# New order lists and buffer places for a fused attention and gated feed-forward kernel on one core

## The chip, the cores and the metric

The kernel runs on one core of a Trainium2 chip. A core has five engines, each with its own instruction queue that runs in order: TensorE (matrix products), VectorE, ScalarE, GpSimd (called POOL in the profile) and SyncE (SP). They wait for each other through semaphores. Transfers between HBM and the on-chip memory SBUF run on 16 DMA engines that all queues share; here POOL and SP issue nearly all of them. Products are written to PSUM, a small memory of 8 banks per partition. The metric is the device time of one execution in microseconds (us); the figure compared is the median over runs.

## The reference

The first half is causal attention, the second a gated feed-forward layer on its result. Cut to what matters:

```python
# q, k, v: [4 batches, 8 heads, 768 tokens, 64]
scores = np.matmul(q, k.transpose(0, 1, 3, 2)) / 8
# heads 0, 2, 6 see all earlier keys; the other five see the
# first 4 keys ("sinks") and the last 64
scores = np.where(mask, scores, -1e9)
a = softmax(scores)
x = np.matmul(a, v)          # as [3072 tokens, 512 features]

g, val = x @ w_gate, x @ w_val            # 512 -> 1536
ffn = (gelu(g) * val) @ w_out             # 1536 -> 512
out = x + sigmoid(x @ w_res) * ffn        # float32 [3072, 512]
```

Inputs are float32; the kernel works in float16 with float32 sums in PSUM.

## The kernel before

**Chunks.** The 3072 tokens are six chunks of 512 (`CHUNKS`); chunks 1 and 4 take the end of one batch and the start of the next. Each chunk goes through loads of q, k and v, a transpose of q and k to put features on partitions, attention scores, exponentials and masks, the weighted sum of v, a transpose of the result, the gate and value products for 12 blocks of 128 hidden features, and output products. The kernel has no loop at run time: every instruction of every chunk is written out, and chunks overlap, so that the attention of one chunk runs between the output products of the one before.

**Transfers.** POOL issues the loads of q, k, v and the weights, which convert to float16 on the way, and for chunks 1 to 4 the stores that add the feed-forward result to `out` (L1523). In the first stages (`loads_rows`) q and k are transposed by TensorE with the identity matrix `ident` (L825). From chunk 2 on (and for four tiles of batch 1) `loads_natural` brings 128 tokens of q or k into a staging buffer `qks` and SP issues a DMA transpose of it (task `dT`, L869), and two copies `q6` (L880) put one head pair on other partitions. For the windowed heads the values are needed a second time, shifted by 64 tokens: that copy `vs` is issued by SP (L774) once the value tiles `va` have landed. From chunk 3 on, half of the attention result is transposed by an SP transpose too (task `xD`, L1217, into `xT`); TensorE transposes the other half (L1226). The attention result itself is stored by SP in one transfer of 1 MB per chunk (`xst`, L1444), before POOL adds to it. The loads of the first chunk come in halves of 256 tokens: of the first half, heads 0 to 3 and 4 to 7 of k and q are four transfers, of the second half k and q are one each.

**Products.** Gate, value and output products use a scheme with seven sub-products in place of eight; their partial sums are added on VectorE (`merge`, `plus`, `s1` to `s4`) and copied by VectorE or ScalarE (`keep`, `seed`, `hold`). A gate or value product of 512 tokens and 512 features is split at its half (`g0`, `v0` and so on, two 512-wide matmuls each): the first half needs the part of `xT` that TensorE transposed, the second half the part that `xD` brings. From the second half of the program on, many products stand as two half-wide matmuls of 64 columns (line L617, the other form is L616). Score tasks (L1013, L1104) and the windowed products (L1137) are blocks of up to 16 small matmuls on parts of the array, and the weighted sums of v (65 columns wide) are small as well.

**The order.** Each piece of work is a task with an engine, a duration in a simple table, dependencies and buffers. A planner (`Graph.schedule`) could place tasks by priority, but here it follows the string `PLAN`. It holds, separated by "/", five lists of task numbers, one for each engine in the order TensorE, ScalarE, VectorE, POOL, SP, and a sixth list that fixes for every buffer which slot (or PSUM bank) it takes, -1 for free choice:

```python
queue = {e: [self.tasks[x] for x in xs] for e, xs in zip(ENGS, lists)}
...
for b, x in zip(bufs, lists[5]):
    b.fixed = x if x >= 0 else None
```

Some tasks may run on more than one engine; the list in which their number stands decides. The planner still walks through modelled time. For a DMA it takes the end as

```python
t.end = dma_free[here] + 1.6 + t.late
```

where `late` is an allowance set where the task is made. In the modelled times where TensorE has nothing to do before the first gate product `g0`, the planner inserts matmuls of a blank tile (task `warm`, L1579 of the profile); they compute nothing that is used. `assign_waits` then gives each task the semaphore waits that its dependencies and the earlier users of its buffers need, and `emit` writes the instructions in the planned order.

Of the kernel before, what the change touches and what calls it, by code (L numbers as in the profile page):

```python
# [54 lines left out]
    "230 242 228 234 408 411 238 232 236 422 240 459 425 414 426 462 427 464 428 432 419 476 467 433 434 442 443 444 445 "  # L55
    "449 451 450 473 440 471 438 457 479 480 481 455 252 482 486 487 488 496 497 498 499 530 522 514 492 503 505 504 494 "
    "538 515 523 509 531 511 546 539 548 558 552 519 534 560 554 518 559 561 553 555 547 570 527 549 526 572 576 542 543 "
    "266 264 250 535 564 566 565 578 567 588 589 582 584 583 590 585 591 676 621 577 579 610 571 573 690 612 613 679 667 "
    "670 614 623 615 616 624 617 672 674 687 625 626 636 696 627 697 692 698 693 699 694 695 628 640 641 683 685 703 704 "
    "705 638 646 714 647 715 713 718 716 717 711 722 709 642 643 724 723 652 653 649 650 730 734 728 655 658 656 741 659 "  # L60
    "740 736 735 742 743 746 737 748 747 749 753 774 785 752 777 754 755 796 788 779 780 799 790 791 782 758 793 801 760 "
    "759 807 802 804 761 818 810 764 829 812 821 766 832 765 823 815 834 813 826 767 824 837 848 835 931 850 852 922 924 "
    "853 854 855 858 859 906 910 861 864 862 865 926 928 867 868 870 871 912 914 881 882 877 934 935 936 937 917 920 933 "
    "938 887 888 879 942 944 943 956 952 953 883 957 958 884 959 954 955 950 948 963 965 964 893 890 894 891 969 971 899 "
    "900 896 897 987 981 975 977 976 978 988 983 982 984 989 1015 990 993 995 999 1018 1026 1037 1020 1001 1029 994 1040 "
    "1021 1023 1032 1031 1042 996 1043 1034 1045 1048 1000 1002 1006 1070 1059 1051 1008 1073 1062 1005 1053 1007 1064 1075 "
    "1056 1065 1067 1054 1078 1089 1166 1076 1091 1163 1093 1094 1153 1156 1095 1099 1100 1096 1105 1106 1102 1103 1147 "
    "1151 1111 1112 1108 1109 1159 1161 1118 1168 1169 1170 1122 1173 1171 1172 1177 1123 1179 1178 1120 1184 1185 1186 "
    "1128 1187 1188 1189 1129 1124 1190 1191 1125 1195 1197 1196 1134 1135 1131 1132 1201 1203 1140 1137 1141 1138 1207 "
    "1208 1210 1209 1213 1219 1221 1220 1222 1247 1215 1214 1216 1250 1226 1269 1258 1252 1253 1225 1261 1255 1272 1227 "  # L70
    "1263 1264 1274 1280 1266 1237 1277 1275 1283 1228 1291 1239 1302 1294 1285 1231 1305 1296 1286 1288 1297 1299 1307 "
    "1233 1308 1310 1321 1402 1232 1234 1238 1240 1385 1323 1325 1326 1379 1383 1327 1331 1332 1328 1399 1387 1337 1338 "
    "1334 1335 1343 1390 1393 1344 1405 1406 1407 1340 1354 1355 1408 1404 1409 1341 1395 1397 1360 1361 1413 1415 1414 "
    "1356 1424 1357 1425 1420 1421 1426 1422 1427 1423 1366 1367 1363 1364 1431 1432 1433 1372 1369 1370 1373 1439 1437 "
    "1350 1449 1450 1443 1444 1445 1446 1456 1451 1452 1461 1483 1455 1463 1486 1494 1457 1488 1458 1497 1462 1464 1505 "
    "1489 1499 1491 1500 1508 1467 1502 1469 1516 1510 1511 1468 1519 1527 1513 1521 1470 1522 1524 1530 1538 1473 1475 "
    "1541 1474 1532 1476 1533 1535 1543 1352 1640 1544 1546 1557 1559 1631 1633 1561 1562 1563 1564 1567 1568 1570 1621 "
    "1623 1571 1573 1574 1635 1637 1576 1577 1579 1580 1615 1619 1590 1591 1586 1626 1629 1643 1644 1596 1597 1645 1646 "
    "1642 1647 1651 1652 1653 1588 1658 1659 1660 1662 1663 1664 1665 1661 1592 1593 1669 1671 1670 1602 1603 1599 1600 "
    "1677 1675 1608 1609 1605 1680 1704 1686 1606 1681 1688 1682 1692 1683 1705 1687 1693 1689 1694 1720 1695 1731 1706 "  # L80
    "1723 1707 1742 1734 1699 1725 1745 1736 1726 1728 1737 1701 1698 1739 1700 1747 1753 1748 1750 1710 1756 1764 1712 "
    "1775 1767 1758 1759 1778 1769 1711 1761 1780 1781 1713 1770 1772 1783 1825 1827 1829 1798 1830 1799 1831 1800 1801 "
    "1832 1835 1836 1804 1805 1838 1839 1807 1841 1808 1842 1844 1845 1813 1814 1847 1848 1794 1810 1811 1796 1816 1817 / "
    "198 229 409 412 237 423 424 460 415 416 465 463 420 477 478 468 226 441 472 474 227 439 513 524 516 532 495 253 512 "
    "540 562 556 520 550 536 528 574 544 267 251 568 580 586 592 258 677 622 611 691 260 680 668 671 261 675 673 688 637 "
    "702 644 684 686 648 639 712 710 645 721 731 729 738 744 750 775 786 756 787 797 798 783 784 762 808 805 806 819 820 "
    "830 1442 831 768 733 828 827 849 932 851 923 925 860 907 911 927 929 913 915 878 918 921 880 941 889 886 949 962 951 "
    "970 972 313 979 985 991 311 1016 997 1027 1038 1028 1025 1024 1003 1047 1046 1049 1071 1072 1061 1009 1069 1068 1090 "
    "1167 1092 1097 1154 1101 1098 1157 1164 1148 1152 1160 1119 1162 1126 1176 1121 1130 1127 1194 1202 1206 365 1211 1223 "
    "1248 1217 1249 1259 1257 1256 1229 1281 1282 1278 1279 1292 1293 1303 1304 1241 1301 1300 1235 1322 362 1403 1386 1324 "  # L90
    "1329 1380 1384 1330 1388 1400 1391 1394 1358 1396 1398 1362 1412 1359 1430 1679 1440 1351 1447 1453 1485 1465 1495 "
    "1459 1496 1506 1493 1492 1471 1517 1518 1515 1514 1529 1539 1540 1477 1536 1537 1353 1641 1558 1560 1632 1566 1634 "
    "1622 1624 1638 1636 1616 1620 1627 1587 1630 1650 1589 1598 1595 1668 1676 1684 1690 1696 1721 1732 1708 1733 1743 "
    "1730 1729 1702 1754 1752 1751 1765 1776 1777 1714 1773 1774 1828 1826 974 1833 1802 1834 1837 1803 1806 1795 1853 1797 "
    "/ 0 15 16 14 17 1 231 243 235 233 239 410 241 224 225 11 413 461 429 13 430 417 418 431 466 421 435 436 446 452 447 "
    "453 437 470 469 448 458 456 454 475 483 489 484 490 485 500 501 506 493 507 502 491 525 12 510 594 517 533 541 595 508 "
    "563 557 521 596 551 545 265 529 598 599 569 537 600 593 587 259 602 601 603 678 575 581 605 632 633 669 606 618 604 "
    "635 681 609 682 689 700 701 629 634 706 607 707 708 719 608 630 720 725 726 654 651 619 727 663 657 664 770 597 660 "
    "771 739 745 772 751 665 776 778 773 789 781 792 800 757 794 803 795 809 763 811 661 814 822 833 825 836 816 769 817 "
    "840 839 838 841 844 842 856 845 857 843 846 847 863 909 866 874 869 875 908 872 885 930 916 939 940 919 945 946 947 "  # L100
    "960 961 966 967 895 892 968 898 1013 1011 1012 901 903 980 986 1014 904 1017 992 1019 312 310 1022 1030 1039 1041 1033 "
    "1044 998 1035 1036 1004 1050 1060 1052 1074 1063 1055 1066 1077 1010 1057 1058 1081 1080 1079 1085 1082 1086 1084 1088 "
    "1083 1087 1107 1155 1104 1115 1116 1149 1150 1110 1113 1158 1174 1175 1180 1181 1165 1182 1192 1193 1198 1199 1136 "
    "1133 1204 1144 1145 1200 1139 1243 1244 1212 1246 1142 364 1245 1224 1218 1251 1270 1271 1254 1260 1262 1273 1265 1276 "
    "1267 1268 1230 1284 1295 1287 1306 1298 1290 1309 1289 1312 1311 1317 363 1236 1318 1242 1313 1314 1316 1320 1333 1315 "
    "1319 1339 1382 1336 1389 1348 1381 1347 1392 1410 1411 1342 1401 1416 1417 1428 1429 1368 1365 1434 1435 1371 1438 "
    "1436 1418 1479 1481 1374 1480 1448 1454 1484 1345 1487 1482 1490 1460 1498 1466 1501 1507 1509 1503 1504 1512 1520 "
    "1528 1523 1472 1526 1525 1531 1542 1534 1478 1549 1545 1550 1377 1376 1548 1551 1547 1553 1565 1554 1552 1555 1569 "
    "1556 1572 1575 1583 1578 1581 1584 1639 1618 1594 1617 1625 1628 1648 1649 1654 1655 1656 1666 1667 1672 1673 1604 "
# [460 lines left out]
def build_kernel(nc, q, k, v, w_gate, w_val, w_out, w_res, out):  # L570
# [153 lines left out]
    def values(b, a, z, base, each, on_engines=False):  # L724

        BB = batch(b)
# [23 lines left out]
        if on_engines:  # L750
            ts = []
# [18 lines left out]
        for lo in cuts:  # L770
            hi = lo + 1 if each else z
            ts = []
            for dst, src, off in ((0, 64, 1), (64, 0, 0)):
# [5 lines left out]
                if on_engines:  # L779
                    ts[-1].late = 1.5  # L780
# [3 lines left out]
    def loads_rows(c, si, b, a, z):  # L784

        BB = batch(b)
# [58 lines left out]
    def loads_natural(c, si, b, a, z):  # L845
# [8 lines left out]
        for i in range(a, z):  # L854
            for j, src in ((1, k), (0, q)):
# [9 lines left out]
                for d in ds:  # L865
                    d.late = 3.5
# [814 lines left out]
```

## Time and profile before

| what | value |
|---|---|
| median of 3 runs | 267.65 us (265.87 to 273.2) |
| the profiled execution | 270.48 us, of it 268.7 us span |
| TensorE busy | 255.6 us, 3434 matmuls |
| VectorE busy | 206.6 us |
| ScalarE busy | 165.6 us |
| POOL busy | 106.6 us, DMA issues included |
| HBM | 29.36 MB read, 10.49 MB written |
| granted TensorE clock, mean | 0.991 |

The span runs from the first to the last instruction; the device time of the same execution is 1.8 us longer. The profile lists groups of instructions by line and tile, the waits of each engine with what ended them, a chain of work that ended last, a timeline, and windows with the busy time of each engine. Lines such as L1217 are those of the kernel before. "PEclk" is the granted clock, 1.00 being full. The queue q0 holds what POOL issued, q1 what SP issued, and q8 the fetches of instructions. "issue" in a wait is time in which an engine waited for no semaphore.

### The profile page before, as it was taken

To read this page: it belongs to the slowest core of one execution; us is meant where nothing else is said; L and a number is where in the kernel's file an instruction comes from. 1 tells how busy PE (TensorE), PEld (TensorE's weight loads), DVE (VectorE), ACT (ScalarE), POOL (GpSimd) and SP (SyncE) were. 2 spreads that over 40 slices of the span, in tenths; PEclk is the share of its full clock that TensorE was granted. 3 is DMA by queue.
4 is the path that set the end of the run, shared out by engine and by line. 5 is a ranking of instruction groups with operands and counts; after the bars stand their busy time and mean duration, and the time that the engine had idled before them with its cause. 6 is when DMAs were issued, how large, how long until landed. Compare 5 with 4: busy or idle time off the path is not lost.

```text
span 268.7 us, 8098 instructions
## 1 busy us (share of the span) xinstructions
PE 255.6 (95%) x3434; PEld 180.5 (67%) x3434; DVE 206.6 (77%) x454; ACT 165.6 (62%) x293; POOL 106.6 (40%) x145
## 2 busy tenths in 40 slices
PE   7899999989999999999999699999999997999992
PEld 5568564458577578577678267589587676778891
DVE  2696566887888978778988567988788985768985
ACT  2588456874655986655886246897365996346421
POOL 8999729803130992769229510001030030110022
PEclk9999999999999999999999799999999999999999
DMA  7999999998989999999909999347473019340004
GB/s 70 171 188 207 181 205 203 157 164 91 166 211 124 165 135 153 115 174 254 168 11 132 169 217 150 72 55 83 165 90 82 2 16 127 46 56 2 2 2 156
DMA packets 102067, 33.17 MB, mean 123 GB/s; under 512 B 88720, under 2 KB 97168, under 8 KB 102032
## 3 DMA queue, kind: packets, MB, share of 16 engines
q0 software_dynamic: 74704, 18.88, 77.2%
q1 hardware_dynamic: 27184, 13.65, 28.6%
q8 instruction: 27, 0.44, 0.7%
q10 hardware_dynamic: 144, 0.13, 0.1%
q14 instruction: 8, 0.07, 0.1%
HBM read 29.36 MB, written 10.49 MB: 148 GB/s over the span
## 4 chain that ended last, share of the span: by engine, by line
PE 70%; DMA 14%; POOL 11%; ACT 2%; issue 2%; DVE 1%; POOLq 0%; DVEq 0%
PE ps L617 32%; PE ps L616 31%; DMA va<-in_v_dram 8%; POOL qks L678 4%; PE ps L1013 3%; DMA xT<-x 3%; DMA vs<-va 3%; POOL va L678 2%; PE ps L1137 1%; POOL wo L678 1%; PE ps L1226 1%; POOL wg L678 1%; POOL wv L678 1%; POOL m_win L636 0%; ACT L1111 0%
## 5 line engine op out<-in xcount | busy, mean ns | idle before, releaser
L1523 POOL DMA_DIRECT2D out_dram<-otile x16 | 14.9, 1014 | 87.8 <-DVE otile L1519 77.6
L616 PE MATMUL ps<-xT,wg 128*128 128x512 f16 (+1 forms) x172 | 40.1, 344 | 0.0
L616 PE MATMUL ps<-xT,wv 128*128 128x512 f16 (+1 forms) x162 | 37.2, 341 | 2.2 <-DMA xT<-x 2.2
L1292 ACT ACTIVATE gact<-ps 128x512 f16<-128x512 f32 x38 | 22.5, 597 | 25.7 <-PE ps L616 17.7
L1294 DVE SCALAR_TENSOR_TENSOR hT<-gact,ps 128x512 f16<-128x512 f16 x38 | 25.8, 685 | 15.0 <-PE ps L616 9.8
L678 POOL DMA_DIRECT2D qks<-in_q_dram x37 | 30.4, 855 | 16.4 <-DMA qT<-qks 8.9
L678 POOL DMA_DIRECT2D qks<-in_k_dram x37 | 31.4, 873 | 10.4 <-DMA kT<-qks 10.4
L678 POOL DMA_DIRECT2D va<-in_v_dram x24 | 23.8, 1014 | 17.0 <-PE ps L1226 11.9
L1366 DVE TENSOR_TENSOR ps<-ps,otile 128x256 f32<-128x256 f32 x60 | 24.7, 429 | 7.2 <-PE ps L616 3.4
L1384 ACT ACTIVATE gact<-ps 128x512 f16<-128x512 f32 x30 | 16.4, 595 | 15.8 <-PE ps L616 8.6
L616 PEld LDWEIGHTS ps<-xT,wv 128*128 128x128 f16 x162 | 15.8, 99 | 14.4 <-DMA xT<-x 2.7
L616 PEld LDWEIGHTS ps<-xT,wg 128*128 128x128 f16 x172 | 16.8, 99 | 10.8 <-issue 1.1
L1029 ACT ACTIVATE ea<-ps 128x1024 f16<-128x1024 f32 (+2 forms) x24 | 21.4, 920 | 3.2 <-PE ps L1013 3.2
L1391 DVE SCALAR_TENSOR_TENSOR hT<-gact,ps 128x512 f16<-128x512 f16 x30 | 19.7, 683 | 1.8 <-PE ps L617 0.7
L617 PE MATMUL ps<-xT,wv 128*64 128x512 f16 (+1 forms) x164 | 20.1, 346 | 0.0
L616 PE MATMUL ps<-wo,hT 128*128 128x256 f16 (+1 forms) x114 | 19.2, 296 | 0.2 <-ACT otile L1490 0.2
L1463 ACT ACTIVATE srs<-ps 128x512 f32<-128x512 f32 x22 | 12.9, 596 | 8.3 <-PE ps L617 7.0
L617 PE MATMUL ps<-xT,wg 128*64 128x512 f16 (+1 forms) x144 | 17.7, 344 | 0.0
L1204 DVE TENSOR_TENSOR xtok<-ps,rcp 128x512 f32<-128x512 f32 (+1 forms) x28 | 16.9, 610 | 0.7
L1495 DVE TENSOR_TENSOR otile<-otile,ps 128x256 f32<-128x256 f32 x33 | 13.6, 417 | 4.6 <-PE ps L617 2.4
L1013 PE MATMUL ps<-qT,kT 64*128 64x64 f16 (+4 forms) x391 | 16.6, 213 | 0.0
L1362 ACT ACTIVATE ps<-ps 128x256 f32<-128x256 f32 x26 | 9.6, 370 | 9.5 <-PE ps L616 6.3
(174 smaller groups left out, 593.5 us busy)
## 6 DMA issues: line engine op xcount, KB each, us to landing
out_dram<-xtok SPq DMA_DIRECT2D x4, 1024.0 KB, 6.3
out_dram<-otile POOLq DMA_DIRECT2D x16, 256.0 KB, 6.0
va<-in_v_dram POOLq DMA_DIRECT2D x24, 128.0 KB, 7.6
qks<-in_k_dram POOLq DMA_DIRECT2D x32, 64.0 KB, 7.6
qks<-in_q_dram POOLq DMA_DIRECT2D x32, 64.0 KB, 7.1
wv<-in_moe_w_val_dram POOLq DMA_DIRECT2D x3, 512.0 KB, 11.3
wg<-in_moe_w_gate_dram POOLq DMA_DIRECT2D x3, 512.0 KB, 7.7
wo<-in_moe_w_out_dram POOLq DMA_DIRECT2D x4, 384.0 KB, 19.7
```

The source lines that it names most:

```text
L616: return e.matmul(o, lhsT=lhsT, rhs=rhs, **k)
L617: return [e.matmul(o[h:h + 64], lhsT=lhsT[:, h:h + 64], rhs=rhs, **k) for h in (0, 64)][-1]
L678: return G.add(eng, issue, lambda e: e.dma_start(out_ap(), in_ap), deps, prio, bufs=bufs, dma=cost, name=name, grp=grp)
L1013: return [e.matmul(at(scr)[:, oo:oo + w], lhsT=side(BB, qb, low, 1)[half, k0:k0 + 128], rhs=side(BB, qb, low, 0)[half, qq:qq + w], start=T ...
L1029: return e.activation(out=o, in_=i_, func=AF.Exp, scale=SM_SCALE)
L1204: t2 = G.add("dve", c_dve(2 * n * 64), lambda e: e.tensor_tensor(out=xview(), in0=avv(0, DHEAD), in1=scale(), op=ALU.mult), [t1] + xdeps, ...
L1292: ta = G.add("act", c_act(512), (lambda gb=gb, ga=ga, gw=gw: lambda e: e.activation(out=at(ga)[:, :], in_=at(gb)[:, gw], func=AF.Gelu))(), ...
L1294: th = G.add("dve", c_dve(512), (lambda vb=vb, ga=ga, f=f, vw=vw: lambda e: e.scalar_tensor_tensor(out=hv(f), in0=at(ga)[:, :], scalar=0.5 ...
L1366: return G.add("dve", c_dve(256), lambda e: e.tensor_tensor(out=at(ps)[:, o], in0=at(ps)[:, BL], in1=at(es)[:, 0:256], op=ALU.add), deps, ...
L1384: ta = G.add("act", c_act(512), (lambda x=x, ga=ga, both=both: lambda e: e.activation(out=two(at(ga)[:, :]), in_=both(x), func=AF.Gelu))() ...
L1391: th = G.add("dve", c_dve(512), (lambda x=x, f=f, ga=ga, both=both: lambda e: e.scalar_tensor_tensor(out=two(hv(f)), in0=two(at(ga)[:, :]) ...
L1523: t = G.add("pool", 1.0, (lambda ot=ot, r0=r0: lambda e: e.dma_start(out[r0:r0 + 128, :], at(ot)[:, :], accum_op=ALU.add))(), ends + [stor ...
```

## The change

The string `PLAN` is replaced, all five lists and the places. Nine values of `late` are raised or set:

```diff
 PLAN = (
-    "230 242 228 234 408 411 238 232 236 422 240 459 425 414 426 462 427 464 428 432 419 476 467 433 434 442 443 444 445 "
...
 )
...
-            BB.vtok[i].late = (0.3 if base < -40 else 1.2) if base < 50 else 4.0
+            BB.vtok[i].late = (1.2 if base < -40 else 1.6) if base < 50 else 4.5
...
-                if on_engines:
-                    ts[-1].late = 1.5
+                ts[-1].late = 2.5
...
-                    t.late = 1.0 if c else 0.0
+                    t.late = 1.0 if c else 0.7
...
-                    d.late = 3.5
+                    d.late = 4.5
...
-                t.late = 1.0
+                t.late = 2.5
...
-            t.late = 1.0
+            t.late = 2.0
...
-        t.late = 2.5 if c == 2 else 1.0
+        t.late = 3.0 if c in (2, 3) else 1.5
...
-        stored[c].late = 1.0
+        stored[c].late = 2.5
...
-                t.late = 2.0 if c < 4 else 1.5
+                t.late = 3.5 if c < 4 else 2.5
```

From the top these belong to the value loads, the shifted copies `vs`, the first loads of q and k, the later loads of q and k, the transposes `dT`, the copies `q6`, the transposes `xD`, the stores `xst` and the accumulating stores. The code of the first loads, with its halves of 256 tokens, is the same in both versions; their order is not. Before, the first six were q of the second half, then q and k of the first half's heads 0 to 3, q and k of its heads 4 to 7, and k of the second half. After, k of the second half comes first, then k, q, k, q of the first half and q of the second. In the new lists 11 more tasks stand on ScalarE and 11 fewer on VectorE, one add of the last chunk stands on POOL, and the program has 68 blank matmuls instead of 70. All lines of the kernel after `PLAN` have numbers lower by one.

## The prediction

> **What bounds the kernel now.** I read the page first, then TensorE's waits, the chain of waits, and around each place that these name the timelines, the windows and the DMA queues. The page's first table and TensorE's own waits:
>
> ```profile
> PE 255.6 (95%) x3434; PEld 180.5 (67%) x3434; DVE 206.6 (77%) x454; ACT 165.6 (62%) x293; POOL 106.6 (40%) x145
> ```
> ```profile
> PE ps L616 <- DMA xT<-x: 2.2, 1, 2.2
> PE ps L1137 <- issue: 2.0, 1, 2.0
> PE ps L1137 <- DMA vs<-va: 1.3, 1, 1.3
> ```
>
> TensorE is the bound: 255.6 of 268.7 us. Three waits make 5.5 us of its idle time; the rest lies before the first load has landed and after the last product. An order of work cannot shorten the products, only these waits. The chain of waits says where they stand (start, us, what):
>
> ```profile
> 31.15 21.46 DMA va<-in_v_dram
> 52.62 7.84 DMA vs<-va
> ...
> 141.83 8.45 DMA xT<-x
> 150.32 9.89 PE ps L616 x50
> ...
> 226.09 1.96 issue
> ```
>
> Wait A, at 59.2: the last value load issued at 31.15 lands at 52.6, its shifted copy takes 7.84, and the windowed product starts at 60.5. Wait B, at 148.1: the DMA transpose xD, issued at 141.83, lands after 8.45 us; TensorE had come to its reader 2.2 us earlier. Wait C, at 225.9: TensorE waits for nothing that has a semaphore. TensorE's timeline there, and the DMA queues from 225.5 to 229:
>
> ```profile
> 225.89 0.19 PE L1137 MATMUL ps<-vs,es 128*64 128x65 f16 x1
> 228.04 0.19 PE L1137 MATMUL ps<-va,es 128*64 128x65 f16 x1 [1.96 <-issue]
> ```
> ```profile
> q8 instruction: 1, 0.02, 1.6%
> ```
>
> A block of sixteen small products stops in its middle while one instruction block is fetched. The windows show what came before it (us, PE busy (x matmuls), clock), beside another dense stretch that ran without a stop:
>
> ```profile
> 181.00:184.62 3.62, 3.62 (x137) 1.00 0.54 55
> 222.66:225.90 3.24, 3.24 (x141) 1.00 1.06 160
> ```
>
> Wait B has a second price. The window after it (PEclk stands behind the POOL pair):
>
> ```profile
> 151.40:154.90 3.50, 3.50 (x10) 1.29 (x9) 2.24 (x5) 1.19 (x2) 0.95 (x2) 0.51 1.72 231
> ```
>
> The clock is at half. In the timeline five groups of two 512-wide products take 3.84 us there (151.20 to 155.04) and 0.435 each elsewhere: 3.84 - 5 x 0.435 = 1.7 us lost. So B costs 2.2 + 1.7 = 3.9.
>
> **What the change does to the program.** I read the orders of both built programs. The planner's lists decide everything: with the new lists and the old values of `late` the emitted program is the new one but for the blank matmuls (70 instead of 68). The nine edits of `late` have therefore no effect at run time of their own. TensorE has the same 732 real tasks; six change between whole and column-halved form. Giving every task its time from this trace (without its waits) the real and blank work adds to 251.6 us before and 251.4 after, 0.2 for two blank matmuls of 0.11. Eleven more tasks stand on ScalarE and eleven fewer on VectorE (293 and 443, from 282 and 454); at 62% and 77% busy both have room. The chains product - ScalarE or VectorE - product are equally tight: in 41 places before and 45 after, less than 0.2 us of other work covers them. I charge 0.5 for these.
>
> *Wait A.* On POOL's queue the four value loads of this stage stand 34th, 37th, 40th and 41st after, and 31st, 43rd, 44th and 46th before. Loads land one behind the other here (the queue carries 189 GB/s from 31 to 53). Two `wo` loads, which landed 1.9 us apart, and two of q and k at 0.3 to 0.5 go behind them: adding the gaps in the new order, the last lands near 47.6, five earlier. With the same 7.84 for the copy that is 55.5, against a need at 59 to 60. Gain 1.3. What is late next are those two `wo` loads: the same sum puts them at 49.4 and 51.4; their readers, at 51.8 and 52.2 before, stand 0.9 us of work later, so nothing waits. If POOL were 4 us later, A would be back.
>
> *Wait B.* From xD's last producer to its first reader TensorE had 7.6 us of work and now has 10.2, because seven first halves of gate and value products go ahead of it instead of two. TensorE asked 6.3 us after xD's issue; now 8.9, against a landing of 8.45: 0.45 to spare. Beside xD, POOL issued eleven loads and four accumulating stores between 139.6 and 155.6; the new list leaves eight loads and four stores there, the other loads going ahead into an idle stretch of POOL (10.1 us before 139.6). So the landing should be shorter. I take the whole 3.9; if it lands 2.6 us later than now, 0.
>
> Here the skill has a rule. "TensorE: Matmul & The Clock Gate", section on HAM oscillation: the clock is halved after idle gaps longer than about 3.4 us. The row shows half clock after 2.2 us of idling. By the rule B is worth 2.2, and any new wait under 3.4 us costs its length alone; by the row B is worth 3.9 and a new wait of 2 us costs up to 3.7. I go by the row, in both directions.
>
> *Wait C.* The densest 128 products in a row take 2.77 us of work before (ending in the stop) and 3.43 after. The second densest stretch before, inside the window 181.00:184.62, also has 3.43, and it did not stop. By these rows C is gone: 2.0. The skill's rule speaks against this part: "Runtime: NRT & Kernel Launch", section on instruction fetch mechanics, says that a block's fetch runs ahead of execution and is mostly hidden; then spreading small products gains nothing. By the rule 0, by the row 2.0. I take 1.6, since 3.43 passed once, on another alignment to the blocks.
>
> *Start.* The first six loads change order (k before q), each with the same 0.73 to 0.95 us issue on POOL; one large load still goes first, and the first transpose still waits for `ident`, written at 6.73. VectorE's ones for the value tiles are done by 2.7, so the value loads' new wait for them costs nothing. Gain 0.2, the two blank matmuls; bounds -1.3 (three gate tasks of 0.43, now ahead of the second half's weighted values, entering idle time) and +1 (a late small load).
>
> *New: the transposes behind xD.* Before, one transpose of the next chunk (of q or k, L869) was ahead of xD on SP's queue and seven behind it until its last reader. Now all eight, and two of the chunk after, stand behind. SP's timeline in this stage:
>
> ```profile
> 143.12 1.87 SPq L869 DMA_TRANSPOSE kT<-qks  x1
> 148.04 0.39 SPq L1444 DMA_DIRECT2D out_dram<-xtok  x1
> 148.48 2.16 SPq L869 DMA_TRANSPOSE qT<-qks  x1
> 150.68 4.04 SPq L869 DMA_TRANSPOSE kT<-qks  x1
> ```
>
> The seven took 2.0 us each on average there (1.2 to 4.05) and landed 4.9 to 11.7 after issue. With A gone xD is issued at 140.5; ten transposes end at 140.5 + 1.25 + 20.2 = 161.9, so the last is issued at 159.9 and, at the seven's mean of 9.1, lands at 169.0. Its reader, a score task, stands 29.9 us of TensorE work behind xD's issue: 170.4. Spare 1.4. For relief, the 1 MB store xst (L1444), between them before, moves behind all of these. Every later product queues behind that score task. Charge 0.5; bounds 0 and, at 2.5 us each (4.8 later, 3.4 of wait, 1.7 of clock), 5.
>
> *End.* One add moves to POOL (0.7) and an output issue stands on ScalarE ahead of a tanh; the add it waits for ends about 0.5 us before that tanh's products do. The last two products and the adds behind them are the same. 0, bounds 0 to +0.5.
>
> **Sum.** The profiled execution took 270.48 (span 268.7 and 1.8 around it): 270.5 - 1.3 - 3.9 - 1.6 - 0.2 + 0.5 + 0.5 = 264.5. Some 0.5 for landings that no row shows gives 265.0. That execution is 2.8 above the median of 267.65 and 4.6 above the fastest, so other runs lack some of A, B and C; the program without them is the same one, and I leave 265.0.
>
> **Rivals.** *The waits are that execution's own.* The fastest run, 265.87, has at most 3 us of the 7.2. Where the median lacks B's 3.9, the change brings 267.65 - 1.3 - 1.6 + 1.5 = 266. For it: the spread of 7.3 us between three runs. With a wait of 2 us and its half clock in the new order it ends at 266 + 3.7 = 269.7. Chance 0.25. *All clean.* Every gain and neither charge, with the start's 1.3: 270.5 - 7.2 - 1.3 = 262.0. Chance 0.12. *Slower.* SP's row of ten transposes: if each takes 3.2 us instead of 2.0, the last comes 12 us later, the score task waits 10.6 us and pays 1.7 of clock: 264 + 12.3 = 276. It decides from 2.9 us each (a wait of 7.3, 273). For it: one took 4.05 in this stage; against it: two took 1.2, and the big store that stood among them is gone. Chance 0.13. The likeliest, near 265: 0.50.
>
> **The numbers.** A measurement of this kernel tells 2% (5.4 us) from no change: 262.3 and 273.0. Faster by more comes from the clean case alone, 0.12; slower 0.13; between 0.75. The range reaches from the clean case, 262.0, over the new wait of the first rival to 271: below it some 0.05, above it 0.15.
>
> **What the profile after would show.** TensorE's waits without `vs<-va` and `xT<-x`, and no `issue` of 2 us; PEclk full through the seventh tenth of the span; the value loads landed by 48; in SP's timeline ten L869 rows behind the first L1217. A wait of L1013 on `kT<-qks` or `qT<-qks` near 170 says that the transposes decide. A stop inside L1137 or L617 beside a q8 packet says that C only moved. I am wrong if TensorE waits in places that none of this names.

## The result and the profile after

The changed kernel takes 263.64 us in the median of 11 runs (262.65 to 265.51); the kernel before took 268.42 beside it (265.87 to 274.85). The ratio is 0.985, with a 95% interval of 0.981 to 0.989: 1.5% faster, which is less than the 2% that count as a difference here. Ratios leave out executions more than 1.5% above the fastest of the same kernel; medians are over all. The forecast was 265.0, with a range of 262 to 271. The profiled execution of the changed kernel took 263.67, its span 261.9.

The page's engine row and clock row, then TensorE's waits (engine, line, what it waited for: us in total, times, longest). All line numbers are lower by one than before:

```profile
PE 253.3 (97%) x3436; PEld 181.4 (69%) x3436; DVE 202.2 (77%) x443; ACT 169.0 (65%) x303; POOL 107.7 (41%) x146
...
PEclk9999999999999999999999999999999999999999
```
```profile
PE ps L1136 <- issue: 1.2, 1, 1.2
PE ps L1578 <- DVE blank L650: 1.1, 1, 1.1
PE ps L824 <- POOL ident L636: 0.6, 1, 0.6
PE ps L824 <- DMA qks<-in_q_dram: 0.6, 1, 0.6
PE ps L616 <- DVE rcp L1190: 0.2, 1, 0.2
```

The waits on `vs` (A) and on `xT` (B) are not there, and the clock is full from the fifth microsecond to the last product. The stop without a releaser (C) is there, at 219.7, with 1.2 us instead of 2.0. The chain of waits and TensorE's timeline at that place:

```profile
215.72 3.92 PE ps L617 x126
219.64 0.09 PE ps L1136 x6
219.73 1.24 issue
220.97 0.35 PE ps L1136 x10
```

It stops once more inside a block of sixteen small products. The windows of the changed kernel where B and its half clock had been (us, then PE, PEld, DVE, ACT and POOL busy with counts; clock, DMA share, GB/s):

```profile
148.10:150.30 2.20, 2.20 (x12) 1.02 (x11) 1.43 (x4) 0.92 (x2) 0.90 (x1) 1.00 2.25 136
151.40:154.90 3.50, 3.50 (x29) 2.66 (x28) 3.07 (x8) 1.92 (x7) 0.06 (x1) 1.00 1.27 222
```

TensorE has no gap, and the second window has 29 matmuls instead of 10. SP's timeline shows why (start, us of issue), and the DMA issues from 138 to 152 give xD's time to landing, that is, until its data have arrived:

```profile
140.16 1.39 SPq L1216 DMA_TRANSPOSE xT<-x  x1
141.60 1.65 SPq L868 DMA_TRANSPOSE qT<-qks  x1
143.29 3.16 SPq L868 DMA_TRANSPOSE kT<-qks  x1
146.50 1.33 SPq L868 DMA_TRANSPOSE qT<-qks  x1
147.88 2.94 SPq L868 DMA_TRANSPOSE kT<-qks  x2
...
154.78 2.72 SPq L868 DMA_TRANSPOSE kT<-qks  x2
```
```profile
xT<-x SPq DMA_TRANSPOSE x1, 5.5
```

xD is issued at 140.16 and lands at 145.68, after 5.5 us instead of 8.45. Its reader starts at 148.48, in TensorE's order and not because of it.

Where the 6.8 us between the two profiled executions (270.48 and 263.67) lie: TensorE's gaps between its first and last product add to 7.1 us before and 2.7 after. Of the 4.4, A is 1.3, B 2.2, C 0.7, and 0.2 lie in all other gaps together. Its busy time is 2.3 shorter: 1.7 by the clock, 0.2 by two blank matmuls, and 0.4 that I did not trace further. The stretch after the last product is 4.8 in both.

### The profile page after: what moved, and what is told of

It reads as the page before. It is cut to its first block, busy times and chain, and to the rows that moved or that the text cites. A ratio compares the mean times of both kernels' runs of the same rounds, so it can differ in the third digit from the quotient of the medians.

```text
span 261.9 us, 8109 instructions
## 1 busy us (share of the span) xinstructions
PE 253.3 (97%) x3436; PEld 181.4 (69%) x3436; DVE 202.2 (77%) x443; ACT 169.0 (65%) x303; POOL 107.7 (41%) x146
## 4 chain that ended last, share of the span: by engine, by line
PE 93%; DMA 2%; DVE 1%; issue 1%; POOL 1%; DVEq 0%; POOLq 0%
PE ps L616 47%; PE ps L617 33%; PE ps L1012 6%; DMA qks<-in_q_dram 2%; PE ps L1136 2%; PE ps L1578 2%; PE ps L1225 2%; PE ps L824 1%; PE ps L1103 1%; POOL qks L678 1%; DVE otile L1518 0%; DVE otile L1528 0%; DVE xtok L1203 0%; DVE ea L1064 0%; DVE rcp L1190 0%
## 5 line engine op out<-in xcount | busy, mean ns | idle before, releaser
L616 PE MATMUL ps<-xT,wg 128*128 128x512 f16 (+1 forms) x172 | 38.7, 337 | 0.0
L616 PE MATMUL ps<-xT,wv 128*128 128x512 f16 (+1 forms) x160 | 35.3, 334 | 0.0
L678 POOL DMA_DIRECT2D qks<-in_q_dram x37 | 31.0, 867 | 6.8 <-PE ps L824 6.8
L1390 DVE SCALAR_TENSOR_TENSOR hT<-gact,ps 128x512 f16<-128x512 f16 x30 | 19.5, 682 | 3.3 <-PE ps L616 1.8
L617 PE MATMUL ps<-xT,wv 128*64 128x512 f16 (+1 forms) x168 | 20.8, 350 | 0.0
L617 PE MATMUL ps<-xT,wg 128*64 128x512 f16 (+1 forms) x144 | 17.4, 344 | 0.0
## 6 DMA issues: line engine op xcount, KB each, us to landing
wo<-in_moe_w_out_dram POOLq DMA_DIRECT2D x4, 384.0 KB, 19.6
```

What stands on the lines that cost most here:

```text
L616: return e.matmul(o, lhsT=lhsT, rhs=rhs, **k)
L617: return [e.matmul(o[h:h + 64], lhsT=lhsT[:, h:h + 64], rhs=rhs, **k) for h in (0, 64)][-1]
L678: return G.add(eng, issue, lambda e: e.dma_start(out_ap(), in_ap), deps, prio, bufs=bufs, dma=cost, name=name, grp=grp)
L1390: th = G.add("dve", c_dve(512), (lambda x=x, f=f, ga=ga, both=both: lambda e: e.scalar_tensor_tensor(out=two(hv(f)), in0=two(at(ga)[:, :]) ...
```

## The experiments

The kernel before was measured anew beside each of five groups of runs, on several chips. Its median lay at 268.4, 269.9, 269.6, 271.8 and 271.6 there, while the changed kernel (measured in the first group) and its variants stayed between 263.3 and 264.8 throughout. So the ratios of different groups differ by 1% through the kernel before alone, and small differences between variants are read from the traces. Each trace is one execution. `PLAN`'s lists are shown as pieces of the list of one engine.

**Wait A alone.** Three value loads go ahead on POOL's list of the kernel before:

```diff
-... 205 206 207 286 209 208 246 257 289 247 404 ...
+... 257 205 206 207 247 246 286 209 208 289 404 ...
```

> The kernel before with three of the value loads of wait A moved ahead on POOL's list, nothing else. Theory (wait A is the last value load): the four land by 48 instead of 52.6, the shifted copies by 56, the wait of 1.3 on vs is gone and the span is 1.3 shorter; 0.995 of the time before. Rival (the wait belongs to the one profiled execution, or the two output-weight loads that now land later take its place): the time stays within 0.3 us, and TensorE waits for wo or for something else between 50 and 62.

The ratio is 0.995 (0.991 to 0.999). TensorE's waits in its profile:

```profile
PE ps L1137 <- issue: 2.0, 1, 2.0
PE ps L616 <- DMA xT<-x: 1.8, 1, 1.8
PE ps L616 <- DVE ps L1366: 1.2, 1, 1.2
```

`vs` is gone from the list; its last copy landed at 57.1, before TensorE came to it. B and C are there as before, and behind B stands a wait of 1.2 us on a merge (L1366) which lasted 0.1 before. What it waits for is told below, with the first run on stop C. The step stands: the wait on `vs` was 1.3 us, and POOL's order alone removes it. Three other executions with the old order of these loads waited 1.1, 1.3 and 1.3 us there.

**Wait B by TensorE's order.** Five first halves of gate and value products go ahead of xD's first reader (tasks 1210 and 1209) on TensorE's list of the kernel before:

```diff
-... 1207 1208 1210 1209 1213 1219 1221 1220 1222 1247 1215 1214 ...
+... 1207 1208 1219 1220 1213 1214 1225 1210 1209 1221 1222 1247 1215 ...
```

> The kernel before with five first halves of gate and value products moved ahead of the first reader of the transpose xD on TensorE's list; POOL's order stays. Theory of the prediction (the order of TensorE's work covers the landing): xD still lands about 8.4 us after its issue, TensorE comes to its reader 8.3 after the issue, the wait shrinks from 2.2 to below 0.3, no half clock follows, and the time falls by 3.9 us (0.985). Rival (what removed the wait in the changed kernel is the faster landing, 5.5 us there): the wait is covered here as well but the landing is 8 us or longer, and the gain is only the 2.2 us. A third case: the landing varies so much that the wait is back.

In the profiled execution there is no wait on `xT` and no half clock (span 266.3); xD landed after 6.8 us this time. Over 12 runs nothing is gained: 1.001 (0.996 to 1.007). The profiled execution, at 268.0, is faster than the median of 269.9, and what the others waited for was not seen. Two places offer themselves: a landing later than the 8.3 us that this order covers, and the merge behind it.

**Wait B by POOL's order.** TensorE's list stays. Seven loads go ahead of the store 1114, for which POOL waited from 129.5 to 139.6:

```diff
-... 905 1114 382 385 358 391 1117 389 361 377 1146 372 ...
+... 905 382 385 358 391 389 361 377 1114 1117 1146 372 ...
```

> The kernel before with seven loads moved ahead of the accumulating store for which POOL waits until 139.6; TensorE's order stays. Theory that the traffic beside xD makes its landing long: it lands in about 5.5 us instead of 8.45, which is before TensorE asks (6.3 after the issue), so the wait and the half clock are gone: 3.9 us less (0.985). Theory of the prediction alone (TensorE's order is what decides): xD lands 7 us or more after its issue, and 0.7 us or more of the wait stays.

xD landed 4.7 us after its issue, and the ratio is 0.992 (0.989 to 0.995), 2.2 us less. The waits:

```profile
PE ps L1137 <- issue: 1.6, 1, 1.6
PE ps L1137 <- DMA vs<-va: 1.3, 1, 1.3
...
PE ps L616 <- DVE ps L1366: 0.2, 1, 0.2
```

A and C are still there, B is gone with two first halves ahead of its reader instead of seven, and the whole interval lies below 1. So what made xD late was in the main the loads that POOL issued beside it.

**Stop C with more work.** The kernel before, with one task of output products (1588, in the dense stretch) executed twice; the second execution gives the same values:

```diff
+                if t.seq in (1588,):
+                    t.fn(engine)
                 res = t.fn(engine)
```

> The kernel before with one task of output products (eight matmuls, 1.03 us, in the dense stretch at 223) executed twice; the second execution overwrites the first with the same values. Theory (the stop of 1.96 us at 225.9 is the fetch of an instruction block that cannot be hidden behind a block of 3.2 us): the block now lasts 4.2 us, the stop shrinks to about 0.9, and the 1.03 us of added work costs nothing: within 0.2 us of the time before. Rival (fetches are hidden and the stop has another cause): the stop stays near 2.0 and the time rises by 1.0 us.

The stop fell from 2.0 to 0.5 (`issue` below; L619 is L617 there, shifted by the two lines). The time, 1.002 (0.997 to 1.007), does not tell 0 from 1.0 us. Nor is the fall the work of the added task alone. By "the block" I mean from here on the 256 instructions of TensorE ahead of the stop, which one fetch brings (see the last section). It lasted 0.6 us more, since the added task pushed other work out of it; the other 0.9 came from a fetch that landed sooner in this execution. Where nothing at this place was changed, the old kernel stopped for 1.6 to 2.0 us. Other waits of the same profile:

```profile
PE ps L618 <- DVE ps L1368: 2.2, 1, 2.2
PE ps L1139 <- DMA vs<-va: 1.3, 1, 1.3
...
PE ps L618 <- DMA xT<-x: 1.0, 1, 1.0
...
PE ps L619 <- issue: 0.5, 1, 0.5
```

The first is a new one: a merge on VectorE. VectorE's timeline says what it waited for:

```profile
159.46 0.42 DVE L1365 COPY otile<-ps 128x256 f32<-128x256 f32 x1 [2.44 <-DMA out_dram<-otile]
159.99 0.77 DVE L1368 TENSOR_TENSOR ps<-ps,otile 128x256 f32<-128x256 f32 x2
```

The copy needs a buffer that POOL's store 1146 still reads, and that store landed at 159.4. When xD lands sooner, TensorE comes earlier to the merge behind that copy and waits there. Store 1146 was issued at 147.7 before, behind the same loads, and landed after 11.9 us; in the run with POOL's order changed only 0.2 of this wait is left. So clearing B on TensorE's side alone need not pay: the next wait has the same cause. That this took the gain from the run with TensorE's order is not shown; in its one profile store 1146 landed after 9.2 us and the merge was not late.

**The lists without the new values of `late`.** The new `PLAN` with the old nine values:

```diff
-            BB.vtok[i].late = (1.2 if base < -40 else 1.6) if base < 50 else 4.5
+            BB.vtok[i].late = (0.3 if base < -40 else 1.2) if base < 50 else 4.0
...
-                t.late = 3.5 if c < 4 else 2.5
+                t.late = 2.0 if c < 4 else 1.5
```

> The new lists and places with the old nine values of late. Theory (the values of late act only in the planner's modelled time): the emitted program is that of the changed kernel with 70 blank matmuls instead of 68; a time within 0.5 us of the changed kernel's, 0.985 of the time before, TensorE stops once near 219.7 for 1 to 2 us. Rival (the allowances change waits or starts of transfers): more than 1 us slower than the changed kernel, with waits on landings.

264.29 us, 0.983 (0.976 to 0.990) of before, and a span of 261.9 as with the new values. One new wait is in its profile, 0.9 us on a value load at 19.6. The loads' order at the start is the same in both, so this is the landing in that execution; it appears in two more runs below. The stop is there with 0.7 us.

**Stop C by spreading.** The changed kernel with output task 1586 moved into the dense block:

```diff
-... 1626 1629 1586 1642 1643 1647 1644 1645 1646 1651 1652 1588 ...
+... 1626 1629 1642 1643 1647 1644 1645 1646 1651 1652 1586 1588 ...
```

> The changed kernel with one task of output products (eight matmuls, 1.03 us) moved from ahead of the dense block of small products into it, nothing else. Theory (the stop of 1.24 us at 219.7 is an instruction fetch that a block of 3.95 us cannot hide; it started 2.6 after the block's begin and took 1.4): the block now lasts 4.7 us, the stop is gone and the time is 1.2 us less than the changed kernel's, 0.981 of the time before. Rival (the stop only moves to the next dense block, or the tanh behind the moved task comes late): time of the changed kernel within 0.4 us, and the stop or a wait on tanh near 218 to 222.

The theory as I had put it failed: the time, 263.89 us and 0.980 (0.973 to 0.987), is that of the changed kernel, and in the profiled execution the stop grew. That execution was the slowest of six (266.21, the others 262.2 to 265.0), so its two waits need not be there in the others.

```profile
PE ps L1136 <- issue: 2.1, 1, 2.1
PE ps L616 <- DMA xT<-x: 1.4, 1, 1.4
```

The block did become longer (4.5 us, not 4.7), but the fetch began 4.5 us after the block's begin, where it had been 2.6. So a fetch's start is not fixed to the block. The second line is a surprise as well: with the new order on POOL and TensorE both, xD landed after 9.8 us here, and TensorE asked after 8.3.

**More work in the changed kernel.** Task 1588 twice, now in the changed kernel, with the same edit as above.

> The changed kernel with one task of output products (1.03 us, inside the dense block that ends in the stop of 1.24 us) executed twice with the same result. Theory of the fetch: the block lasts 5.0 us, the stop falls from 1.24 to 0.2 or less, and 1.03 us of added work costs nothing: the time of the changed kernel within 0.3 us. Rival (the stop has another cause): the stop stays and the time is 1.0 us above the changed kernel's.

The stop fell from 1.2 to 0.4, and 263.69 us, 0.981 (0.975 to 0.987), is the time of the changed kernel, although TensorE has 1.03 us more work. The block is 0.6 us longer, not 1.0, and the rest is again a fetch that landed sooner. Five runs with this block unchanged and all its stores, or two of them, stopped for 0.7 to 1.5 us.

**TensorE's order undone.** xD's readers go back behind two first halves in the changed kernel:

```diff
-... 1219 1213 1138 1207 1214 1208 1220 1225 1209 1210 1215 ...
+... 1138 1207 1208 1210 1209 1219 1213 1214 1220 1225 1215 ...
```

> The changed kernel with the first readers of the transpose xD moved back to where they stood before on TensorE's list, behind two first halves instead of seven; POOL's order stays new. Theory after the first runs (POOL's order decides how soon xD lands): TensorE asks about 6.2 us after the issue, xD lands 5.5 after it, no wait, and the time stays that of the changed kernel within 0.5 us. The prediction's own theory (the seven first halves cover the landing): TensorE waits 1 to 3 us on xT, in part with half clock, and the time rises by 1 to 4 us.

264.74 us in the median of 4 runs (262.77 to 266.48), 0.984 (0.976 to 0.993). xD landed after 7.1 us; TensorE asked after 6.2 and waited 0.9. The time does not tell the two theories apart; the wait says that both are part of it. With POOL's new order the landings of xD over seven runs are 5.0, 5.5, 5.6, 5.7, 7.1, 7.9 and 9.8; two first halves cover four of them, seven cover all but the last.

**POOL's order undone.** In the changed kernel store 1114 goes back ahead of five loads:

```diff
-... 354 347 358 382 391 1114 371 372 1117 ...
+... 1114 354 347 358 382 391 371 372 1117 ...
```

> The changed kernel with the accumulating store of 138.5 moved back ahead of five loads on POOL's list, so that twelve loads instead of seven stand behind it, as before the change; TensorE's order stays new. Theory (POOL's order decides how soon xD lands, and the seven first halves cover at most 8.3 us of it): xD lands 7 to 10 us after its issue, TensorE waits 0 to 1.5 us on xT, and the time rises by 0.5 to 2 us. The prediction's own theory (the seven first halves cover it): no wait, the time of the changed kernel within 0.4 us.

264.41 us (262.84 to 267.65). xD landed after 8.4 us, and TensorE asked then: no wait. The time does not tell the two theories apart. But two other lines moved:

```profile
PE ps L1136 <- issue: 1.5, 1, 1.5
...
PE ps L1012 <- DMA kT<-qks: 0.6, 1, 0.6
```

The last of the transposes behind xD landed at 169.0 here, and the score task waited 0.6 us for it. That is the mechanism of the slower rival, at the place it named, for a small price. In the changed kernel the same transpose landed at 162.3.

**One store less beside the dense block.** If the fetch's start is not fixed to the block, something delays it. With the begins of the blocks counted back from the stop, fetches that met POOL's traffic mostly started late and others mostly did not. Three accumulating stores of 256 KB run from 213.5 to 222.5. One of them was ready at 204.4:

```diff
-... 1375 1585 1378 1582 1614 ...
+... 1375 1378 1585 1582 1614 ...
```

> The changed kernel with one accumulating store of 256 KB, whose data are ready at 204.4, moved ahead of the one for which POOL waits until 213.5; nothing else. Theory (an instruction fetch comes late when POOL's stores hold the DMA engines: over ten traces its start lies 2.6 us behind the block's begin in the median with such traffic and 0.1 without; three stores of 256 KB run from 213.5 to 222.5): two stores instead of three beside the dense block, the fetch starts 0.5 to 1.5 us sooner, the stop of 0.7 to 1.2 us at 219.7 falls below 0.4, and the time is 0.8 us less than the changed kernel's (0.981 of the time before). Rival (the fetch's start has nothing to do with the stores): the stop stays between 0.7 and 1.3 and the time is the changed kernel's.

263.46 us, the stop unchanged at 1.2, the fetch 3.1 us after the block's begin. By itself that speaks against the stores. But the two that were left kept POOL's queue busy through the first 3 us of the block, so the fetch met the same traffic as before.

**Both stores away.** The last of the three now also waits for the last small product of the block:

```diff
-... 1375 1585 1378 1582 1614 ...
+... 1375 1378 1585 1582 1614 ...
...
+    G.tasks[1582].deps.append(G.tasks[1665])
     span = G.schedule()
```

> The changed kernel with two of the three accumulating stores taken away from the dense block: the one that is ready at 204.4 goes first on POOL's list, and the last of the three, which began at 215, now also waits for TensorE's last small product of the block (219.3); its buffer is used again at 232.8 only. Theory (a fetch comes late while POOL's stores hold the DMA engines): from 217.1 to 219.3 no store is in flight, so the fetch starts by 217.3 and lands by 218.4, the stop of 1.2 us at 219.5 is gone, and the time is 1.1 us less than the changed kernel's (262.5). Rival, after the run with one store moved, which changed nothing (the fetch's start does not depend on the stores): the fetch starts 2.5 to 3.2 us after the block's begin again, the stop stays between 0.7 and 1.3, and the time is the changed kernel's (263.6).

All of TensorE's waits in this run:

```profile
PE ps L616 <- DMA va<-in_v_dram: 1.4, 1, 1.4
PE ps L1578 <- DVE blank L650: 1.1, 1, 1.1
PE ps L616 <- DVE rcp L1190: 0.2, 1, 0.2
```

No stop. The DMA queues during the same 256 instructions, first of the changed kernel (215.5 to 219.6), then of this run (216.46 to 220.41):

```profile
DMA  4889699998959919686449499999948378499799
...
q0 software_dynamic: 308, 0.57, 98.5%
q8 instruction: 1, 0.02, 2.2%
```
```profile
DMA  9407979799361006000000000000000000000000
...
q0 software_dynamic: 96, 0.16, 25.0%
q8 instruction: 1, 0.02, 1.6%
```

With the queue empty after a third of the block, the fetch began 1.5 us after the block's begin and landed 1.4 before its end. The time is 263.28 us, 0.976 (0.969 to 0.982); that is 0.4 below the changed kernel's median and not told from it, since a wait of 1.4 on a value load at 19.5 stands in its profile instead. It is the lowest median of all versions, but I don't call it faster.

**Three moves on POOL's list alone.** The kernel before with the moves of the first and third experiment and, in the same way, store 1378 ahead of 1582 and 1585:

```diff
-... 383 1375 1582 1585 1378 1614 ...
+... 383 1375 1378 1582 1585 1614 ...
```

> The kernel before with three moves on POOL's list alone: the three value loads (wait A), the seven loads ahead of the store at 139.6 (wait B), and the accumulating store that is ready at 210.5 ahead of the one for which POOL waits until 219.6 (the stop C). TensorE's order and all others stay. Theory (what the change gained came from POOL's list): no wait on vs, none on xT above 0.3, a stop below 1.0, and 4 us or more less than before, at the changed kernel's time (0.985). Rival (other parts of the new lists carry a share): the time stays 1.5 us or more above the changed kernel's (0.991).

264.71 us (263.47 to 265.46), 0.978 (0.973 to 0.984), where two variants of the changed kernel measured beside it had 0.974 and 0.976. Its waits:

```profile
PE ps L1137 <- issue: 0.8, 1, 0.8
...
PE ps L616 <- DVE ps L1366: 0.4, 1, 0.4
```

Neither `vs` nor `xT` is among them, the merge behind store 1146 still costs 0.4, and the stop fell from 2.0 to 0.8 with the fetch 1.9 us after its block's begin. Three moves on one queue bring all but about 1 us of what the whole change brought.

## Why the prediction was right, and where it was not

Its sum went from 270.5 by 5.5 to 265.0; the same two executions differ by 6.8. That the sum comes so near is in part luck: C gave 0.9 less than was taken for it, and the three charges of 0.5 did not come. Step by step:

- **Wait A, 1.3.** Right, with its times: the last value load landed at 48.05 (47.6 forecast), the two `wo` loads behind at 49.3 and 51.2 (49.4 and 51.4), and nothing waited for them. Alone it gave 0.995.
- **Wait B, 3.9.** The size was right in these two executions, 2.2 and 1.7, but they are not typical: with the old order xD was waited for 1.8 and 1.0 us in two other executions, without half clock behind it. The cause was half wrong. The step gave the gain to TensorE's seven first halves, which were to cover a landing of 8.45 with 0.45 to spare, and named POOL's shorter row only in passing. TensorE asked 8.3 us after the issue and not 8.9, so that a landing of 8.45 would have been 0.1 late. In the runs TensorE's order alone gained nothing that could be measured, and POOL's gained 2.2 us. With POOL's new order xD mostly lands before TensorE asks even in the old order; the first halves cover the late landings, up to 8.3 us. The step also lacked a term: store 1146, late behind the same loads, holds the copy that the merge needs, at 0.1 to 2.2 us.
- **Half clock.** The prediction went by the row (half clock after 2.2 us of idling) and not by the rule of the Trainium skill ("TensorE: Matmul & The Clock Gate", section on HAM oscillation). The row was the better guide: in the run with 1.0 us on `xT` the clock was halved after the 2.2 us on the merge instead. What the row did not say is that the place of a wait counts as well; see the last section.
- **Stop C, 1.6 of 2.0.** Mis-sized: 0.7 was gained. The step took a stretch of 3.43 us that had not stopped as proof that 3.43 is long enough, and lowered the gain only because of another alignment. That stretch does not lie inside the window named: the 128 densest products near it run from 182.7 to 186.1, across two blocks. The block that begins at 181.0 lasted 3.6 us; the one that stopped lasted 3.2 before and 3.95 after. And at 181.0 no store was moving data yet and the fetch came 0.7 us after the block's begin; here the stores were moving data and it came after 2.6. The length of the block was one of two numbers. The skill's rule that a fetch is mostly hidden ("Runtime: NRT & Kernel Launch", section on instruction fetch mechanics) fits every block here but this one.
- **Start, 0.2.** Two blank matmuls, 0.2; the gaps of the first 25 us are 2.4 and 2.3 us.
- **The transposes behind xD, +0.5.** Nothing: the ten took 1.6 us each instead of 2.0, the last was issued at 156.1 (159.9 forecast) and landed at 162.3, 5.7 before its first reader. With POOL's order undone it was 0.6 late. The step had the right risk and put too little of it on POOL.
- **Tight chains +0.5, landings +0.5.** Gaps below 0.3 us add to 0.3 less, not more; no landing but those named showed up in this execution. In three later runs a value load at 19.5 cost 0.3, 0.9 and 1.4; the start had been given +1 at most.
- **The rivals.** That the waits were that execution's own is true in part: the median fell by 4.8 and not by 6.8, because the profiled execution of before lay 2.1 above its median and that of after at its own. The clean case (262.0) came closest to these two profiles, 263.7; what kept it away was C.

## What to carry over

Before work is moved ahead of a late transfer, look at what is in flight beside that transfer and why it is in flight then: here POOL stood 10 us before one store with its loads queued behind, and then sent all of them beside the transpose that TensorE needed next. A wait that is shortened at the waiting engine can uncover the next one with the same cause; clearing the queue removed the first here and most of the second. An instruction stop needs two things, a block with little work and a late fetch. Here moving work in did not remove it and taking traffic away did, each in one trace; what that is worth in time was not told from nothing.

## What the runs showed of the hardware

**When an instruction stop comes.** A fetch is 16 KB. The 27 fetches of the changed kernel's page (0.44 MB) stand for 6,872 products and weight loads and 79 semaphore instructions, 257 for each, which I take as 256 instructions of 64 bytes. The stop belongs to a place in the instruction stream: in all thirteen traces that stopped, of both kernels, it comes after TensorE's 5,825th recorded instruction, semaphore instructions included. Counted back 256 products and weight loads from the stop, in us:

| run | block lasts | fetch starts after its begin | fetch takes | stop |
|---|---|---|---|---|
| before | 3.23 | 3.10 | 0.92 | 1.96 |
| output task twice, before | 3.81 | 1.24 | 1.87 | 0.5 |
| three moves on POOL | 3.23 | 1.93 | 0.96 | 0.8 |
| after | 3.95 | 2.57 | 1.44 | 1.24 |
| output task moved in | 4.48 | 4.52 | 0.93 | 2.11 |
| output task twice, after | 4.52 | 2.75 | 0.96 | 0.4 |
| one store less | 3.95 | 3.11 | 0.92 | 1.2 |
| both stores away | 3.95 | 1.50 | 1.01 | 0 |

In each row that stopped, the stop is the sum of the two fetch columns less the block, plus 1.1 to 1.2; in the last row this is below zero. The dense stretch at 181 of the kernel before fits: 0.74 and 0.96 plus 1.2 less 3.63 is below zero. That POOL's traffic delays the start is shown for this block by the last run: 1.50 lies below the 2.55 to 4.52 of the six traces of the changed kernel with three stores. In the three runs with fewer stores the queue's last packets beside the block ended at 2.3, 3.4 and 1.3, and the fetch began within 0.4 us of that. By how much a given store delays it is open: with the same stores the fetch began at 4.5 in one run and 2.6 in another, and before at 3.10 and, amid the traffic, at 1.24.

**The clock goes by fixed windows.** In all fourteen traces the changes of the granted clock lie on a grid: full for 146.773 us, half for 3.413, full for 112.640, which are 43, 1 and 33 times 3.4133; 256.000 in the changed kernel is 75 times. The grid's begin differs by execution. TensorE's busy share in the window ahead went with it: 0.36 (before, the wait of 2.2 at 148) and 0.36 (output task twice, 2.2 on the merge) were followed by half clock, 0.41, 0.45, 0.48 and 0.56 were not. The window rows of the second case:

```profile
157.30:160.70 3.40, 1.21 (x10) 0.65 (x8) 1.14 (x3) 1.57 (x3) 0.00 (x0) 1.00 1.62 161
160.70:164.20 3.50, 3.50 (x17) 2.21 (x15) 1.65 (x5) 0.75 (x2) 0.00 (x0) 0.51 1.36 187
```

So 2.2 us of idling inside one window cost 1.7 more, and waits of 1.8 to 2.1, or C of before, which the grid cut in two, cost their length alone. One case does not fit: a window at 10.7 with 0.66, in small products (in the run with A alone), was followed by half clock too. The rule is drawn from few windows, and its threshold lies somewhere between 0.36 and 0.41 here.

**One transfer, twofold time.** With the same lists of POOL and SP xD took 5.0 to 9.8 us to land from one execution to the next.
